# Eight of the q transposes move from TensorE and ScalarE to a crossbar DMA on SyncE, with a new order table

## The chip, the cores and the metric

The kernel runs on one core of a Trainium2 chip. The metric is the device time of one execution in microseconds (us). The engines are named as in the profile: PE is TensorE (PEld is its weight load), DVE is VectorE, ACT is ScalarE, POOL is GpSimd, SP is SyncE. PE, DVE, ACT and POOL compute; SP only issues DMAs here, and ACT and POOL issue some as well.

## What is computed

A linear attention over 8 batches, 8 heads, 576 positions and 64 channels per head feeds a channel mix with 512 model channels and 1024 hidden ones. The inputs and the output are float32; the matmuls run in bfloat16.

```python
# attention: q, k, v are [8, 8, 576, 64]
q_s = softmax(q, axis=-1)            # over the 64 channels
k_s = softmax(k, axis=2)             # over the 576 positions
kv  = einsum('bhsd,bhse->bhde', k_s, v)
x   = einsum('bhsd,bhde->bhse', q_s, kv)        # then [8, 576, 512]
# channel mix
x_prev = x shifted by one position (a zero in front)
xk = mu_k * x + (1 - mu_k) * x_prev
xr = mu_r * x + (1 - mu_r) * x_prev
k  = relu(xk @ w_k)                  # [.., 1024]
out = sigmoid(xr @ w_r) * (k * k @ w_v)
```

## The kernel before

The kernel is a list of some 950 operations (`Op`), each with an engine, what it depends on and which buffers it takes and gives. A long string, `ORDER` (L42 to L115), names all of them in one sequence; `Plan.ordered` (L149) emits them in that sequence. Each engine then runs its own operations strictly in the order in which the table has them, and waits at an operation until its inputs are there. The number after a colon is the buffer that the operation takes. `ACT!load00k0` puts a DMA on ACT's queue. So the table decides what stands behind what on every engine and on every DMA queue, and nothing is reordered at run time.

The names are made of a kind and indices. For the attention the indices are batch and group of four heads (two groups a batch), so `qt41` is batch 4, group 1:

- `load41q0`, `load41k0`, `load41v0`: the loads (L189 to L205), for batches 1 to 7 on POOL's queue.
- `expq`, `rsum`, `rrec`, `scale` (L419 to L422): exp of q on ACT, then row sums, reciprocals and the scaled softmax on DVE, which writes q into a tile `qs` [128, 9, 128]: a partition holds one head of a pair and one of 64 rows of positions, the free dimension nine blocks of 128 channels (two heads of 64).
- `expk`, `cast` (L423, L425): exp of k and the cast of v, on ACT.
- `B41` (L440 to L448), one block on PE with three parts in a row: x of the head group before it (`x`, L512 to L519, which reads that group's transposed q from `qt` and its weights `w`), the transposes of this group's q (`transpose_q`, L356 to L363: for batches 4 to 7 36 matmuls of 64 by 64 against an identity, into PSUM), and this group's `kv` (L383 to L392). `TKV20` and `TKV30` are blocks without the first part; for the two groups in `ALONE` the x is a block of its own (`X21`, `X71`).
- `rz`, `w` (L451, L506) on DVE: one over the sum of exp(k), and the weights kv over it.
- `qt41` (L507, `copy_qt` L365 to L372): ACT copies the transposed q from PSUM into the SBUF tile `qt` [128, 2, 640]. It waits for `B41` and for `w41`, and gives the PSUM pair back.
- `xs`, `xb` on ACT, `edge`, `diff`, `sc`, `mix` on DVE (L521 to L556): x out of PSUM, its shift and the two mixes xk and xr.

The channel mix runs over 10 units of 512 positions (two of them, units 4 and 9, of 256), index first: `k46` is unit 4, hidden block 6 (L598; four matmuls, PE), `relu46` (ACT) and `sq46` (DVE) follow it; `r40` and `th40` are the gate of unit 4, tile 0 of 128 positions (L630, PE; tanh on ACT); `v400` and `v401` are the two halves of its second matmul (L650, PE, four matmuls each); `o40` multiplies the two (L657, DVE) and gives `th`, of which there are 7 buffers; `st40` and `st40.2` store its two halves of 64 positions from SP's queue (L662). Of the last unit, `v910`/`v911` and `v910.2`/`v911.2` are the two column halves of the last tile, `o91` and `o91.2` their gates; for the last two tiles the second store of each pair (`st90.2`, `st91.2`, `st91.4`) is issued by ACT (L680).

Batches 0 and 1 are treated in another way (`FUSED`: the mixing factors are put into the weights); the change doesn't touch them, nor batches 2 and 3, except for their places in the table.

Of the kernel before, what the change touches and what calls it, by code (L numbers as in the profile page):

```python
# [38 lines left out]
ALONE = ((2, 1), (B - 1, 1))  # L39
FIRST = ((0, 0), (0, 1), (1, 0), (1, 1))  # L40

ORDER = """  # L42
ACT!load00q0:0 zero ident load00q1 ACT!load00k0:1 load01q1:2 ACT!load01q0 rows load00v consts warm
load00k1 load01v late load01k0:3 load10q0:4 wk00 load11q0:5 expq001:0 wk01 expq000 rsum001:0 wk10
rsum000 expk000:0 wk11 ACT!load01k1 rrec001 rrec000 scale001:0 expq011:1 scale000 fill:1 fill.2:2
fill.3:3 fill.4:0 fill.5:1 fill.6:2 fill.7:3 fill.8:0 fill.9:1 fill.10:2 fill.11:3 fill.12:0
fill.13:1 fill.14:2 fill.15:3 fill.16:0 wide:0 expq010 rsum011:1 fill.17:1 fill.18:2 T00:0 rsum010
expk001 load10q1 rrec011 rrec010 scale011:1 widecopy fill.19:3 KV001:1 qt00:0 KV000 scale010 Z00
fill.20:1 fill.21:1 T01:3 rz00:0 rest expk010:1 kvn00:0 expk011 edge00 load10k0:6 fill.22:1
KV010:2 wp000:0 expq100:2 wp001 wr X000:0.1 qt01:1 KV011 x0001 Z01 load11q1 x0000 rz01:1 X001:1.3  # L50
kvn01:1 load10v1:7 edge01 k00:0 wp010:1 x0010 k02:1 x0011 expq110:0 X010:0.1 wv0 k01:2 x0100 x0101
k03:3 wp011 load10k1 k00.2 k02.2 relu00:0 k03.2 load10v0 relu02:1 k01.2 relu03:2 k05:0 load11v0:8
sq02:0 sq00 relu01:1 load11v1 k04:1 relu05:0 sq01 expq101 rsum100:2 k07:3 expk100:2 rrec100 sq03
X011:0.1 relu07:1 load11k1:9 k06:2 x0110 x0111 load11k0 relu04:2 sq05 r03:0 scale100:2 relu06:0
wv1 expq111 rsum101 r00:3 cast101:0 rsum111:3 r02:1 th03:0 rrec111 th00:1 rrec101 rsum110 r01:2
th02:2 wv2 rrec110 expk101 v020:0 sq04 load20v0:10 scale111:0 cast100 v030:3 load20q0:0 scale101
th01:3 sq07 muload v000:1 cast110:1 scale110 cast111 TKV10:0 expk111:0 load21q0:2 v010:2 rz10:2
expk110 kvn10:0 sq06 qt10:2 wp100:0 TKV11:1 v021 rz11:0 kvn11:1 v011 qt11:0 wp110:1 wp111 v001
# [12 lines left out]
rz30:0 k23:2 sc2111:1 st10 sc2110 st10.2 th20:1 mix211 load50k0:3 k22:0 cast400:0 w30:2 o13 k27:3
relu23:2 scale310:1 load61q0:8 st13 k24:1 relu22:1 st02.2 qt30:2 st13.2 k21:2 rsum400:0 st01
relu24:0 k20:0 st12.2 expk400:2 sq22:0 st12 mix201 B31:0.1 relu21:1 sq24 load51k0:9 r22:1 xs30:1
rz31:1 sq23 relu27:0 rrec400 w31:0 relu20:2 r23:2 scale400:2 xb30 k25:3 qt31:1 sq27 edge30 k26:0
sq21 diff30:0 relu25:0 B40:1.0 relu26:1 sc3001:2 sq25 expq410:0 r21:3 sq20 rz40:2 w40:1 th23:6
sq26 load71k0:1 v230:0 rsum410:1 th21:2 th22:0 v200:2 xs31:0 xb31 sc3000 v220:3 sc3011:1 sc3010
mix300 qt40:0 r30:1 edge31 diff31:1 expq500:1 v201 sc3101:0 v221 sc3100 th30:4 load51v0:2 mix310
cast410:1 v231 o22 expk410:0 k35:1 sc3110:2 load61k0:6 o23 k33:3 rrec410 st23.2 relu35:0 o20
load70v0:0 expq510:2 rsum500:2 k30:0 st20.2 st11.2 k41:1 load70q0:7 st01.2 sq35:1 v210:2 relu41:2
sc3111 st23 cast500:2 scale410:0 k37:1 relu33:1 load70k0:4 v211 mix301 relu37:0 expk500:1 k32:3  # L80
sq41:0 o21 k40:1 expq600:0 sq37 load60k0:3 st21 k31:2 sq33 st21.2 rrec500 mix311 relu40:2 B41:0.1
load71v0:10 relu31:0 rsum510:3 relu32:1 r32:1 sq40 sq32 r33:2 relu30:2 rrec510 scale500:1 th32:3
r31:3 xb40:1 sq30 k36:0 xs40 sq31 th31:6 edge40 scale510:2 k34:1 relu36:1 k47:3 relu34:2 diff40:0
v310:0 th33:2 sq34 expk510:2 v330:1 rz41:0 sc4001:0 w41:2 sc4010:1 v300:2 relu47:0 sq36 load71q0:9
rsum600:0 k46:3 v331 relu46:2 cast510:0 sq46 k44:3 sc4000 rrec600 v311 mix400 relu44:1 load61v0:2
qt41:2 scale600:0 k43:3 v301 expq610:1 o31 B50:1.0 relu43:2 o30 r41:0 sc4011 xs41:0 st30.2 rz50:1
xb41 sq47 w50:0 st31 k42:3 st31.2 v320:2 edge41 relu42:0 st11 diff41:1 qt50:1 st30 k45:3 sq44
sc4101:2 st20 v321 cast600:1 o33 sc4100 B51:0.1 sq43 relu45:1 mix410 cast610:2 r40:1 sq42 rz51:2
sq45 o32 expq700:2 k52:3 rsum610:1 th41:6 k50:2 relu52:2 sc4111:0 k51:0 rrec610 relu50:0 rsum700:2
expk600:0 v410:3 sq52:1 k53:2 relu51:1 sc4110 w51:1 expk610:1 sq51 v411 mix411 relu53:2 k54:0 o41  # L90
xb50:0 sq50 v400:2 scale610:1 relu54:1 k55:3 expq710:0 rrec700 mix401 v401 relu55:0 rsum710:3
th40:5 k56:0 qt51:0 k57:3 sq53 sq54 relu56:2 r50:1 sq55 relu57:1 scale700:2 r51:0 th50:4 cast700:0
rrec710 v500:3 o40 sq56 st40 v510:1 th51:1 sq57 st41 xs50 edge50 B60:1.0 st33 diff50:0 st32.2 v501
st41.2 xb51:1 sc5000:2 rz60:0 sc5001 st40.2 w60:2 v511 mix500 xs51 qt60:2 o50 r52:2 expk700:2 o51
st50 B61:0.1 edge51 st50.2 sc5010:0 expk710:0 diff51:1 st22 v520:0 st51 sc5011 th52:6 sc5100:1
st51.2 r53:3 sc5101 cast710:1 sc5110:2 mix510 v521 sc5111 th53:5 rz61:1 mix511 v530:1 o52 xb60:1
k60:2 w61:0 st52 mix501 qt61:1 v531 st32 scale710:0 st52.2 k61:3 relu60:0 st22.2 xs60 o53 B70:1.0
relu61:2 sq60:0 st53 edge60 k62:0 st53.2 diff60:0 xb61:0 st33.2 sq61 k63:2 sc6000:1 relu62:1
sc6001 sc6010:2 xs61 k64:1 mix600 relu63:0 sq62 k65:3 relu64:2 edge61 sq63 diff61:1 k66:0 relu65:1
sq64 k67:2 sc6100:0 relu66:0 sc6101 sq65 r60:1 mix610 relu67:2 sq66 r61:3 th60:4 sc6011 sq67  # L100
# [12 lines left out]
sq94 k97:2 relu96:0 sq95 r90:1 relu97:2 sq96 sq97 r91:0 th90:5 v900:3 th91:2 v901 v910:2 o90 v911
st90.2 st90 v910.2:1 o91 v911.2 st91.2 st91 o91.2 st91.4 st91.3
"""  # L115


class Slot:

# [698 lines left out]
```

## Time and profile before

| | |
|---|---|
| median of 3 runs | 198.74 us (198.21 to 198.87) |
| the profiled execution's own time | 198.64 us |
| its span, first to last instruction | 196.9 us |
| DVE busy | 150.6 us (77%), 347 instructions |
| ACT busy | 147.0 us (75%), 224 instructions |
| POOL busy | 43.5 us (22%), 70 instructions |
| DMA bytes moved | 40.13 MB, HBM read 33.56 MB, written 9.44 MB |
| mean granted clock of PE | 0.995 |

What lies around the span is 198.64 - 196.9 = 1.7 us. DVE and ACT are busy over 90% of most of the first two thirds and much less in the last third; the DMA engines are full up to about 75 us, and again in part up to 95 us, and carry little but stores after that.

### The profile page before, as it was taken

What the parts mean: (1) busy time and instruction counts of PE and PEld (TensorE: products, weight loads), DVE (VectorE), ACT (ScalarE), POOL (GpSimd) and SP (SyncE); (2) the same over time, 40 slices, a digit from 0 to 9 for tenths busy, and PEclk for the clock granted to TensorE, in tenths of its full rate; (3) what the DMA queues carried; (4) which work ended last, traced back from release to release, by engine and by line L of the source; (5) the groups of instructions that cost most, each with busy time, mean ns of one, the idle gap of its engine ahead of it and who ended that gap; (6) DMA issues with size and microseconds to landing.
All of it is one profiled execution on the core that took longest, in us unless ns stands there. A gap on an engine that the chain in (4) does not pass through costs nothing.

```text
span 196.9 us, 5187 instructions
## 1 busy us (share of the span) xinstructions
PE 189.0 (96%) x2089; PEld 92.4 (47%) x2089; DVE 150.6 (77%) x347; ACT 147.0 (75%) x224; POOL 43.5 (22%) x70
## 2 busy tenths in 40 slices
PE   7799999999999999999999999999999999999992
PEld 3263445444544554454455445554444544444751
DVE  1985796899999899999799999999725459622531
ACT  3786989899999999998789997986525762652440
POOL 8533456983415202440110000000000000000000
PEclk9999999999999999999999999999999999999998
DMA  6999999999999997799284004653044013403413
GB/s 201 307 294 263 269 358 307 390 384 389 416 392 394 403 409 291 176 410 415 56 268 114 0 0 114 158 127 89 3 107 107 0 42 70 107 0 87 97 34 107
DMA packets 16544, 40.13 MB, mean 204 GB/s; under 512 B 2300, under 2 KB 5640, under 8 KB 16520
## 3 DMA queue, kind: packets, MB, share of 16 engines
q0 software_dynamic: 9440, 27.99, 43.1%
q1 hardware_dynamic: 6264, 10.36, 19.5%
q10 hardware_dynamic: 816, 1.44, 2.0%
q8 instruction: 16, 0.26, 0.5%
q14 instruction: 8, 0.07, 0.1%
HBM read 33.56 MB, written 9.44 MB: 218 GB/s over the span
## 4 chain that ended last, share of the span: by engine, by line
PE 66%; DMA 15%; DVE 8%; ACT 4%; POOL 3%; issue 1%; SPq 0%; DVEq 0%; POOLq 0%; ACTq 0%
PE mm_c L652 10%; PE mm_d L652 8%; PE mm_d L600 7%; DMA wk_bb<-in_moe_w_k_dram 7%; PE mm_a L600 6%; PE mm_c L600 5%; PE mm_b L632 5%; DMA raw_h<-in_v_dram 5%; PE mm_b L600 5%; PE mm_a L652 5%; DMA out_dram<-th_c 4%; PE mm_a L632 4%; PE mm_b L652 3%; PE mm_d L632 2%; PE att_b L390 1%
## 5 line engine op out<-in xcount | busy, mean ns | idle before, releaser
L652 PEld LDWEIGHTS <-k_a 128*128 128x128 bf16 x144 | 13.7, 98 | 16.6 <-DMA wv_a<-in_moe_w_v_dram 0.4
L652 PEld LDWEIGHTS <-k_b 128*128 128x128 bf16 x152 | 14.3, 98 | 14.4 <-issue 0.8
L632 PEld LDWEIGHTS <-xr 128*128 128x128 bf16 x144 | 13.6, 98 | 15.6 <-DVE xr L488 0.2
L632 PE MATMUL mm_b<-wr,xr 128*128 128x512 bf16 x56 | 14.4, 380 | 0.0
L600 PEld LDWEIGHTS <-wk_ba 128*128 128x128 bf16 x80 | 7.7, 98 | 9.1 <-issue 0.8
L600 PEld LDWEIGHTS <-wk_ab 128*128 128x128 bf16 x80 | 7.7, 98 | 8.2 <-issue 0.8
L600 PEld LDWEIGHTS <-wk_bb 128*128 128x128 bf16 x80 | 7.8, 98 | 7.7
L600 PEld LDWEIGHTS <-wk_aa 128*128 128x128 bf16 x80 | 7.5, 98 | 8.2 <-issue 0.7
L632 PE MATMUL mm_a<-wr,xr 128*128 128x512 bf16 x36 | 9.3, 380 | 0.0
L652 PE MATMUL mm_c<-wv_a,k_a 128*128 128x512 bf16 x32 | 8.2, 379 | 0.0
L591 DVE TENSOR_TENSOR k_b<-rel_b 128x512 bf16<-128x512 bf16 (+1 forms) x15 | 6.0, 402 | 2.1 <-ACT rel_b L587 1.8
L600 PE MATMUL mm_d<-xk,wk_ba 128*128 128x512 bf16 (+1 forms) x28 | 7.3, 341 | 0.3 <-ACT rel_a L587 0.3
L591 DVE TENSOR_TENSOR k_a<-rel_b 128x512 bf16<-128x512 bf16 (+1 forms) x13 | 5.2, 398 | 3.0 <-ACT rel_b L587 3.0
L600 PE MATMUL mm_d<-xk,wk_bb 128*128 128x512 bf16 (+1 forms) x28 | 7.3, 341 | 0.0
L632 PE MATMUL mm_d<-wr,xr 128*128 128x512 bf16 x28 | 7.2, 379 | 0.0
L587 ACT ACTIVATE rel_c<-mm_b 128x512 bf16<-128x512 f32 (+1 forms) x7 | 3.6, 509 | 4.7 <-PE mm_b L600 4.7
L600 PE MATMUL mm_c<-xk,wk_aa 128*128 128x512 bf16 (+1 forms) x24 | 6.9, 371 | 0.0
L600 PE MATMUL mm_c<-xk,wk_ab 128*128 128x512 bf16 (+1 forms) x24 | 6.9, 370 | 0.0
L587 ACT ACTIVATE rel_a<-mm_b 128x512 bf16<-128x512 f32 (+1 forms) x7 | 4.2, 593 | 3.6 <-PE mm_b L600 3.6
L591 DVE TENSOR_TENSOR k_a<-rel_c 128x512 bf16<-128x512 bf16 (+1 forms) x14 | 5.2, 372 | 1.9 <-ACT rel_c L587 1.9
L600 PE MATMUL mm_a<-xk,wk_aa 128*128 128x512 bf16 (+1 forms) x22 | 6.4, 370 | 0.1
L600 PE MATMUL mm_a<-xk,wk_ab 128*128 128x512 bf16 (+1 forms) x22 | 6.3, 369 | 0.1
(346 smaller groups left out, 545.9 us busy)
## 6 DMA issues: line engine op xcount, KB each, us to landing
raw_d<-in_k_dram POOLq DMA_DIRECT2D x4, 576.0 KB, 10.0
out_dram<-th_g SPq DMA_DIRECT2D x14, 128.0 KB, 2.4
raw_c<-in_q_dram POOLq DMA_DIRECT2D x3, 576.0 KB, 9.8
raw_h<-in_q_dram POOLq DMA_DIRECT2D x3, 576.0 KB, 9.9
out_dram<-th_a SPq DMA_DIRECT2D x10, 128.0 KB, 7.3
out_dram<-th_b SPq DMA_DIRECT2D x10, 128.0 KB, 2.4
out_dram<-th_e SPq DMA_DIRECT2D x10, 128.0 KB, 2.4
raw_k<-in_v_dram POOLq DMA_DIRECT2D x2, 576.0 KB, 7.9
```

The costliest lines, as they stand in the source:

```text
L390: kn.nc.tensor.matmul(kn.half(slot, r)[two[u], KVO:KVO + n], lhsT=kn.eks[ek.index][two[r], j, u, :], rhs=by, start=(j == 0), stop=(j == J ...
L587: kn.nc.scalar.activation(out=kn.rels[rel.index][:, 0:n], in_=kn.bank(kf)[:, 0:n], func=ACT.Relu, scale=HALF_ROOT)
L591: kn.nc.vector.tensor_tensor(out=kn.k2s[k2.index][:, fc, 0:n], in0=kn.rels[rel.index][:, 0:n], in1=kn.rels[rel.index][:, 0:n], op=ALU.mult)
L600: kn.nc.tensor.matmul(kn.bank(kf)[:, 0:n], lhsT=kn.wk[fc // 4][ct % 2][:, ct // 2, (fc % 4) * 128: (fc % 4) * 128 + 128], rhs=kn.xs[0][:, ...
L632: kn.nc.tensor.matmul(kn.bank(rps), lhsT=kn.xs[1][:, ct, c:c + 128], rhs=kn.wr[:, ct, :], start=(ct == 0), stop=(ct == CT - 1))
L652: kn.nc.tensor.matmul(kn.bank(vps)[:, 0:width], lhsT=kn.k2s[k2.index][:, ft, 128 * m:128 * m + 128], rhs=wv_of(ft)[:, part], start=(ft == ...
```

## The change

For batches 4 to 7 (`CROSSBAR`, eight head groups) the transposes leave the PE block, and ACT's copy `qt` is replaced by one DMA on SP's queue, which reads the whole tile `qs` [128, 9, 128] and writes its nine 128 by 128 blocks transposed into the tile `qt`. The DMA waits for the scaled q (`scale`) and for the `qt` buffer. The PE block no longer waits for `scale`; the block that reads the transposed q, the next one of the list, now waits for the DMA. The PSUM pair is given back by `w` instead of by the copy. The layout of the transposed tile differs: x of these groups reads eight runs of 64 columns, 128 elements apart, instead of 512 columns in a row. The table `ORDER` is new as a whole; in it most stores stand right behind their `o`.

```diff
+CROSSBAR = tuple((b, g) for b in range(4, B) for g in range(2))
 ORDER = """
...
+qt41:2 r31:1 sq31:0 relu37:2 o20 st20 st20.2 k32:3 rz41:0 sq35
+th31:2 rsum500:2 k33:0 relu32:1 xb40:1 k46:2 w41:2 sq37 k30:1 sq32 xs40 relu33:0 edge40 k40:3
+rrec500 rsum510:3 r32:0 relu40:2 relu30:1 k34:3 th32:5 sq30 sq33 B50:0.1 diff40:0 relu34:1 k42:1
...
+v821 relu96:2 v830:0 o82 st82 st82.2 sq95 v811 sq96 v800:3 o81 st81 st81.2 sq92 v831 v801 v910:2
+o80 st80 st80.2 v900:1 o83 st83 st83.2 v910.2:3 v911 v901 v911.2 o90 o91.2 st90 o91 st91.2 st91
+st90.2 st91.4 st91.3
 """
...
+        def qt_crossed(t):
+            return t[:].rearrange("p r c -> p (r c)")[:, 0:2 * S].rearrange(
+                "p (j c) -> p j c", c=128)
...
+        crossed = (b, g) in CROSSBAR
...
-                transpose_q(qtp)
+                if not crossed:
+                    transpose_q(qtp)
                 kv(qtp)
...
-                tr = kvm = add("PE", block, before_t + before_kv + turn_x[1] + alone, [qtp] + turn_x[2], [qs] + leave_kv + turn_x[3], name=f"B{tag}")
+                tr = kvm = add("PE", block, ([] if crossed else before_t) + before_kv + turn_x[1] + alone, [qtp] + turn_x[2], ([] if crossed else [qs]) + leave_kv + turn_x[3], name=f"B{tag}")
...
-        wdone = add("DVE", lambda: weights(kvp, kn.ws[w.index]), [zdone], [w], [rz], name=f"w{tag}")
-        qcopy = add("ACT", lambda: copy_qt(qtp), [tr, wdone], [qt], [qtp], name=f"qt{tag}")
+        wdone = add("DVE", lambda: weights(kvp, kn.ws[w.index]), [zdone], [w], [kvp, rz] if crossed else [rz], name=f"w{tag}")
+        if crossed:
+            qcopy = add("SP", lambda: kn.nc.sync.dma_start_transpose(
+                out=qt_crossed(kn.qts[qt.index]),
+                in_=kn.qss[qs.index][:].rearrange("p j d -> p (j d)")), scaled, [qt], [qs],
+                name=f"qt{tag}")
+        else:
+            qcopy = add("ACT", lambda: copy_qt(qtp), [tr, wdone], [qt], [qtp], name=f"qt{tag}")
...
+        def x_columns(r, u, at, n):
+            t = kn.qts[qt.index]
+            if crossed:
+                return qt_crossed(t)[two[u], at // 64:(at + n) // 64, 64 * r:64 * r + 64]
+            return t[two[u], r, 64 + at:64 + at + n]
```

The end of the table before reads `v900 th91 v901 v910 o90 v911 st90.2 st90 v910.2 o91 v911.2 st91.2 st91 o91.2 st91.4 st91.3` (buffer numbers left out).

More of the change, by code (lines that the diff above doesn't have):

```diff
@@ L39 @@
 ALONE = ((2, 1), (B - 1, 1))
+CROSSBAR = tuple((b, g) for b in range(4, B) for g in range(2))
 FIRST = ((0, 0), (0, 1), (1, 0), (1, 1))
 ORDER = """
[L43 to L46, printed above, removed]
@@ L53 @@
[L53 to L58, printed above, removed]
@@ L71 @@
[L71 to L100, printed above, removed]
@@ L113 @@
-sq94 k97:2 relu96:0 sq95 r90:1 relu97:2 sq96 sq97 r91:0 th90:5 v900:3 th91:2 v901 v910:2 o90 v911
-st90.2 st90 v910.2:1 o91 v911.2 st91.2 st91 o91.2 st91.4 st91.3
+ACT!load00q0:0 zero load00v load00q1 ACT!load00k0:1 load01q1:2 ident ACT!load01q0 rows
+ACT!load00k1 load01k0:3 load01v consts warm load10k1:4 late wk00 load10q1:5 expq001:0 load01k1
+expq000 wk01 rsum001:0 rsum000 wk11 expq011:1 rrec001 expk000:0 wk10 rrec000 scale001:0 fill:1
+fill.2:2 fill.3:3 fill.4:0 fill.5:1 fill.6:2 fill.7:3 fill.8:0 fill.9:1 fill.10:2 fill.11:3
@@ new lines @@
+relu01:1 k03.2 X011:1.0 load10k0 relu03:2 k07:0 load10v0 x0110 x0111 expq100 sq01:0 k05:1 sq02
+relu00:1 k04:3 sq00 relu05:0 relu07:1 load11v0:9 r00:2 sq05 expq110:0 load11k0 r01:1 expq111
+load11v1 r02:0 th00:0 rsum111:3 wv1 cast101:0 r03:2 rrec111 relu04:0 rrec101 sq03 rsum110 th01:1
+k06:3 th02:2 rrec110 scale101:2 th03:3 v010:1 wv2 relu06:2 rsum100 expk111:0 v030:0 load20v0:10
+rrec100 sq04 expk100 sq07 muload v020:2 scale100 cast100 v000:3 scale111:0 cast110:1 load20q0:0
+scale110 TKV10:0 expk110 load21q0:2 sq06 cast111 rz10:2 load30q0:1 kvn10:0 qt10:2 TKV11:1 v001
@@ new lines @@
+mix210 v131 rz30:0 o10 cast310:2 load70v0:7 sc2110:0 k23:2 st10.2 o13 st12 load50v0:10 sc2111
+k27:1 relu23:1 st02 scale310:1 th20:4 st02.2 k20:3 relu27:2 st03.2 w30:2 cast400:0 k21:2 st12.2
+sq27:0 sq23 mix201 k24:0 qt30:2 load50k0:0 rsum400:0 k26:1 relu21:0 relu20:2 B31:1.0 mix211
+expk400:2 rrec400 k22:2 sq20 rz31:1 relu24:1 sq21 load51v0:8 scale400:2 relu26:2 k25:3 relu22:0
+r22:0 xs30:0 w31:0 xb30 qt40:0 sq24 sq22 r23:1 qt31:1 edge30 r21:2 diff30:0 th22:2 st01 sc3001:2
+B40:0.1 th21:3 sq26 sc3010:1 v220:0 relu25:1 sc3000 th23:6 sq25 r30:2 expq410:0 sc3011 mix300 v221
@@ new lines @@
+xs31:1 rsum410:1 load60q0:5 xb31 v230:3 th30:1 edge31 v210:1 cast410:1 diff31:1 v231 rz40:2
+sc3101:0 expq500:1 load60k0:3 sc3100 o22 st22 st22.2 v211 expk410:0 mix310 load71v0:4 v200:2 w40:1
+sc3110:2 expq510:2 st10 k35:0 o23 st23 st23.2 load71k0:1 o21 st21 st21.2 v201 load61q0:9 relu35:0
+sc3111 cast500:2 mix311 k31:3 rrec410 mix301 k41:1 expk500:1 load61v0:10 B41:1.0 scale410:0 k37:0
+relu41:2 load70k0:0 relu31:1 sq41:1 qt41:2 r31:1 sq31:0 relu37:2 o20 st20 st20.2 k32:3 rz41:0 sq35
+th31:2 rsum500:2 k33:0 relu32:1 xb40:1 k46:2 w41:2 sq37 k30:1 sq32 xs40 relu33:0 edge40 k40:3
@@ new lines @@
+st33 st33.2 relu45:0 expq700:2 rsum610:1 k53:2 k52:1 rrec600 sq42 sq47 relu53:2 k55:3 sq45
+scale600:0 relu52:1 v410:2 relu55:0 rz51:2 cast600:1 sc4110:0 k51:1 mix401 sq52:0 k57:3 o32 st32
+st32.2 relu51:1 v411 sq55 expq710:0 sc4111 sq53 k54:0 sq51 xs50:1 qt51:0 relu57:0 o41 st41 st41.2
+k50:1 xb50 mix411 rsum700:2 k56:3 relu50:2 r40:2 relu56:1 rrec700 edge50 r50:1 w51:1 th40:0 sq50
+diff50:0 r51:3 rsum710:3 r53:2 qt60:2 th51:6 relu54:2 sc5011:1 B60:0.1 sq57 sc5010 v500:3 xs51:0
+sq56 th50:4 sq54 xb51 rz60:0 r52:0 sc5001:2 v400:1 edge51 th52:5 diff51:1 cast610:2 v501 sc5000
@@ new lines @@
+rrec710 rrec610 v530:0 w60:2 th53:3 mix501 cast700:0 v510:2 mix500 sc5100:0 expk610:1 v401
+sc5111:1 sc5101 o50 st50 st50.2 v511 sc5110 mix510 v531 o40 st40 st40.2 k63:3 o53 st53 st53.2
+scale610:1 k62:1 relu63:0 expk700:2 k61:0 o51 st51 st51.2 qt61:1 k60:3 cast710:1 scale700:2
+B61:1.0 relu61:1 sq63:1 v520:2 relu62:2 qt70:0 rz61:1 sq61 relu60:0 scale710:0 k64:0 xb60:1 k67:1
+mix511 xs60 w61:0 k66:3 relu67:1 B70:0.1 sq67 qt71:2 edge60 sq60 r60:1 xs61:0 relu64:1 rz70:2
+w70:1 xb61 v521 sq64 sq62 diff60:0 th60:1 k65:0 edge61 o52 st52 st52.2 r62:1 relu65:0 sc6010:2
@@ L517, in x @@
                                             lhsT=kn.ws[w.index][two[u], r, :],
[L518 removed]
+                                            rhs=x_columns(r, u, at, n),
                                             start=True, stop=True)
```

66 lines of the change are left out of this document (35 added, 31 removed).

## The prediction

> **What bounds the kernel now.** I read first the busy shares, then the 40 slices, PE's waits, the stretches of 5 us, and the timeline of one block that the change touches.
>
> ```profile
> PE 189.0 (96%) x2089; PEld 92.4 (47%) x2089; DVE 150.6 (77%) x347; ACT 147.0 (75%) x224; POOL 43.5 (22%) x70
> ...
> PE   7799999999999999999999999999999999999992
> ```
>
> PE is busy in all slices but the first two and the last. Its waits between 33 and 190 us are two:
>
> ```profile
> PE mm_d L600 <- ACT rel_a L587: 0.3, 1, 0.3
> PE att_b L390 <- ACT ek_a L325: 0.3, 1, 0.3
> ```
>
> So from 33 us on PE's own work sets the end: a microsecond of PE work taken out there is a microsecond gained, and a new wait of PE there is lost in full. Before 33 us the loads set the pace. The end of the chain of waits into block TKV11 shows it: ACT's last exp follows the loads, and PE waits for it.
>
> ```profile
> 31.45 0.58 ACT ek_a L325
> 32.05 0.69 ACT ek_a L325
> 32.79 0.48 PE att_b L390 x36
> ```
>
> **What is removed: PE.** One block, B50 (start, duration, instruction):
>
> ```profile
> 100.01 0.22 PE L516 MATMUL att_b<-qt_c,w_c 64*64 64x64 bf16 x4
> 100.06 0.39 PE L516 MATMUL att_a<-qt_c,w_c 64*64 64x512 bf16 x4
> 100.28 0.46 PE L360 MATMUL att_b<-ident,qs_b 64*64 64x64 bf16 x36
> 100.56 0.48 PE L390 MATMUL att_b<-vv_c,ek_b 64*64 64x65 bf16 x36
> 100.97 1.04 PE L632 MATMUL mm_a<-wr,xr 128*128 128x512 bf16 x4
> ```
>
> Matmuls are pipelined, so a part costs the distance of the starts, not its duration: the 36 transposes cost 100.56 - 100.28 = 0.28 us. The eight blocks (starts at 71.55, 87.31, 100.28, 104.81, 120.55, 124.36, 131.59 and 156.10) give 0.28 to 0.30 each, in sum 2.29 us, all in the stretch where PE has no gaps. Gain: 2.29 us, certain to within 0.1.
>
> **What is removed: ACT.** Eight copies like this group's:
>
> ```profile
> L368 ACT COPY qt_a<-att_b 128x1152 bf16<-128x1152 bf16 x4 | 4.6, 1152 | 1.3 <-DVE w_b L407 1.1 <-DVE kvn_b L407 0.2
> ```
>
> 8 x 1.13 = 9 us of ACT, and its wait for `w` (1.1 us once). I count it at 0: PE's work covers ACT, and it waited 0.3 us for ACT in 157 us. If a dearer order needed ACT sooner it could be worth those 0.3 us.
>
> **What is added: eight transposing DMAs.** The trace has none. Each moves 128 x 1152 x 2 = 288 KB within SBUF. The nearest rows, from issue to landing:
>
> ```profile
> out_dram<-th_a SPq DMA_DIRECT2D x10, 128.0 KB, 7.3
> out_dram<-th_b SPq DMA_DIRECT2D x10, 128.0 KB, 2.4
> ...
> raw_f<-in_q_dram POOLq DMA_DIRECT2D x2, 288.0 KB, 10.9
> ...
> raw_c<-in_q_dram SPq DMA_DIRECT2D x1, 288.0 KB, 4.7
> ```
>
> Bounds: not under 2.4 us (a store of under half the bytes, alone) and, by the same bytes in a crowd of loads, up to 10.9. Alone on the DMA engines I take 3.3 us: 2.4 plus 160 KB at 204 GB/s, the page's mean (0.8; rounded up). Beside loads, as up to 95 us, I take 6 us: stores of 128 KB in flight between 78 and 95 us have medians of 3.3 to 7.5, several queued at once, and this one stands nearly alone with over twice the bytes.
>
> The Trainium skill speaks for both ends. "DMA: Bandwidth & Descriptors" (section "Latency and other measured facts") has 261 GB/s for a transposing DMA, an estimate of 1.1 us for these bytes plus the fixed part. "VectorE: DVE Perf Modes" (section "The three transpose paths") has 1,309 ns for one 128 by 128 block by DMA against 390 on TensorE, and advises TensorE where PSUM will do; nine blocks one after another would be 11.8 us. No run here shows either; the second is the case of the slow transposes below.
>
> **How much time each transpose has.** A full PE step (four matmuls of 512 columns) is 0.86 us, a half one 0.44, by the chain of waits. DVE steps there: scale 1.27, mix 0.67, o 0.59, sc 0.28, rrec 0.17. The new table's own sequences tell which is short.
> - qt61 stands on SP behind the stores of o51. From the end of v531 DVE has o53, scale610, o51: 0.59 + 1.27 + 0.59 = 2.45 us. PE has k63, k62, k61, k60, k64, k67, k66 and then B70, which reads qt61: 7 x 0.86 = 6.0. Left: 3.6 us.
> - qt41 waits for scale410. From the end of v211 DVE has up to mix310, w40, sc3110, o23, o21, sc3111, mix311, rrec410, mix301, scale410, some 5.4 us; PE has five steps of which one is half (3.9), B41 (0.68 without transposes) and k37, r31, k32, k33, k46, k30, k40, r32, k34 (6.9) before B50: 11.5. Left: 6.1 us, at about 83 to 89 us, beside the last loads.
> - qt51 stands behind the stores of o32, about 5.5 us ahead of B60 (k50, k56, r40, r50, r51, r53 and a little). The others have 6 to 15 us, by the PE steps between.
>
> At 3.3 us alone and 6 us beside loads all fit, by 0.3 and 0.1 us. So: 0, with 0.1 us for the narrow ones. Each microsecond more costs one at B70 and one at B50; from 5.5 us on a third at B60. At the low bound still 0.
>
> **What is moved.** SP issues 85 DMAs instead of 77: the eight are added and each holds the queue for 0.5 to 1.7 us (the issues of stores). Queued behind a waiting transpose are stores, and for them only the next tanh on one of 7 `th` buffers waits; two stores take 2.4 us and a tile 3 PE steps. I count 0; if the queue jams by 5 us, a tanh comes late and PE with it. The 1 us of DMA time each is 8 us of 16 engines that carry 85 GB/s after 95 us.
>
> x reads eight runs of 64 columns instead of 512. Low bound 0; high, if each run costs as the matmuls of 64 columns above do (0.05 for four), 8 x 0.05 against 0.22, 0.18 x 8 = 1.4 us. I take 0: the same columns stream, in the same number of matmuls.
>
> **The start and the middle under the new table.** Up to TKV11 the new sequence on POOL brings the same loads, only load11v1 last instead of load11k0, and PE has the same steps to do; one cast instead of two exps stands behind the last load. I take 0, with -0.7 to +0.7. From there to B31 the PE steps are the same in number. A new table may leave PE gaps that no row tells: 0 to 2 us.
>
> **The end.** Start, duration, instruction of the last microseconds:
>
> ```profile
> 192.55 0.38 PE L652 MATMUL mm_b<-wv_c,k_b 128*128 128x256 bf16 x2
> ...
> 192.64 1.40 ACTq L668 DMA_DIRECT2D out_dram<-th_c  x2
> 192.97 0.42 DVE L658 SCALAR_TENSOR_TENSOR th_c<-th_c,mm_b 128x256 f32<-128x256 f32 x1 [0.40 <-PE mm_b L652]
> ```
>
> PE ends at T = 192.93; one half-width o follows (to T + 0.46), then the last issue (0.70, the second of the two), and it lands 2.2 us after that (the median of these stores), at T + 2.7. The new table ends PE with v901, v911.2 and DVE with o90, o91.2, o91, in this order: v901 is done 0.44 before T, o90 (0.69) runs to T + 0.3, o91.2 to T + 0.6, o91 to T + 1.0. ACT then issues st91.2, st90.2, st91.4 one after another, 0.70 each: the last at T + 2.4 at most, landed at T + 4.4 or a little later. Loss: 1.7 us (1.3 to 2.1).
>
> **Sum**, against the profiled execution's 198.64 (0.1 under the median of 198.74): 198.64 - 2.29 + 1.7 + 0.1 = 198.15, and with the 0.1 of the median about 198.2. Under 0.3% (0.6 us) a measurement of this kernel can't be told from no change; this sits 0.5 below the median.
>
> **The rivals.**
> 1. *The transposes come late* (slower). Place: B70 and B50, which wait for qt61 and qt41, with all of PE behind them. It decides from 3.6 us alone and 6.1 beside loads. At 5 us and 7.5: 1.4 + 1.4, 198.2 + 2.8 = 201.0; a range of 199 to 202. For it: margins of 0.3 and 0.1 us, and stores beside loads take up to 7.5. Against: from 95 us on the DMA engines are mostly free.
> 2. *The transposes go block by block*, at the 10.9 us of the highest row: B50 4.8, B60 5.4, B70 7.3 late, 198.2 + 17.5 = 215.7; at 8 us 207. Against: nothing else in the kernel is as slow with so little queued.
> 3. *The gain stays whole*: the end costs less (o91 not held by o90, ACT's issues closer) and ACT's freed 9 us close PE's small waits: 198.7 - 2.3 + 0.8 - 0.3 = 196.9. For it: ACT is full up to 95 us. Against: in-order queues at the end.
> 4. *Gaps of the new table* of 1 to 2 us elsewhere on PE: 199.2 to 200.2.
> That the change doesn't do what it says is excluded: PE's program has 288 matmuls less.
>
> **How the numbers follow.** Forecast 0.45 (own range 197.6 to 198.9), rival 1 0.25, rival 2 0.08, rival 3 0.12, rival 4 0.10. Faster by over 0.3% (below 198.14): half of the forecast's case (0.22) and rival 3: 0.34. Same: the other half less its edge, 0.2, and the mild parts of 1 and 4, 0.08: 0.28. Slower: 0.38. The range reaches from rival 3 to the upper part of rival 1: 197.0 to 201.6, which leaves out rival 2 and a few hundredths below.
>
> **What would show it.** B blocks of batches 4 to 7 at 0.68 us instead of 0.96. Transposes landing in 3.3 us alone; if 5 or more, the starts of B70 and B50 show PE waiting for them. The last landing 4.4 us after PE's last matmul. It is wrong if PE has new waits over 1 us between 33 and 190 us that no transpose explains, if x (L516) takes more than 0.27 a block, or if the start shifts TKV11.

## The result, and the profile after

The changed kernel takes 206.76 us (median of 4 runs, 206.35 to 207.11) where the kernel before took 198.60 (198.21 to 198.87): a ratio of 1.041, with a 95% interval of 1.038 to 1.044. It is slower by 8.2 us, and lies 5 us above the upper end of the predicted range. The profiled execution took 206.64 us, its span is 204.9. Medians here and below are of all runs of a kernel, while ratios leave out the runs that are over 1.5% above its fastest.

First the page of the changed kernel: the busy shares, PE's row and the row of its granted clock in 40 slices of 5.1 us, and the DMA packets.

```profile
PE 190.4 (93%) x1801; PEld 92.5 (45%) x1801; DVE 149.3 (73%) x346; ACT 137.1 (67%) x217; POOL 43.7 (21%) x70
...
PE   7789999999999899991999999999999999999980
...
PEclk9957999999999999998599999999999999999996
...
DMA packets 26013, 42.44 MB, mean 207 GB/s; under 512 B 11772, under 2 KB 15112, under 8 KB 25992
```

The last two of these rows in the kernel before:

```profile
PEclk9999999999999999999999999999999999999998
...
DMA packets 16544, 40.13 MB, mean 204 GB/s; under 512 B 2300, under 2 KB 5640, under 8 KB 16520
```

PE has 288 instructions less (2089 to 1801), as it should, and yet 1.4 us more busy time, since it ran at a lower clock in the third and fourth slice and in the 19th and 20th. In the 19th it is nearly idle. The small packets went from 2300 to 11772: 9472 more, 1184 for each of the eight new DMAs.

PE's waits from 25 to 200 us, longest first (what waited, for what, us in total, times, longest):

```profile
PE att_a L536 <- DMA qt_c<-qs_a: 4.7, 1, 4.7
PE att_b L536 <- ACT qt_c L374: 0.6, 1, 0.6
```

The first is block B50, which waits for the transpose qt41. The timeline of PE there (start, duration, instruction, idle time before it):

```profile
97.52 0.27 PE L536 MATMUL att_a<-qt_c,w_c 64*64 64x64 bf16 x4 [4.65 <-DMA qt_c<-qs_a]
97.55 0.67 PE L536 MATMUL att_b<-qt_c,w_c 64*64 64x512 bf16 x4
97.96 0.75 PE L396 MATMUL att_a<-vv_c,ek_b 64*64 64x65 bf16 x36
98.64 0.61 PE L620 MATMUL mm_b<-xk,wk_aa 128*128 128x256 bf16 x2
...
99.47 0.64 PE L620 MATMUL mm_a<-xk,wk_ba 128*128 128x256 bf16 x2
...
100.32 0.63 PE L620 MATMUL mm_d<-xk,wk_ba 128*128 128x256 bf16 x2
```

Between x (L536) and kv (L396) nothing stands any more: the transposes are gone. But behind the wait PE runs at half its pace. Three half-width k steps start at 98.64, 99.47 and 100.32, 0.84 us apart; at full clock such a step takes 0.44. The busy time in stretches of 5 us shows the granted clock (third number from the end) beside it:

```profile
90.00:95.00 5.00, 2.86 (x16) 1.37 (x14) 5.00 (x11) 2.85 (x7) 0.00 (x0) 1.00 1.03 318
95.00:100.00 5.00, 2.48 (x51) 1.85 (x51) 0.97 (x4) 0.84 (x3) 0.00 (x0) 0.60 1.04 298
100.00:105.00 5.00, 5.00 (x23) 2.59 (x22) 1.62 (x4) 3.31 (x6) 0.72 (x1) 0.72 0.22 43
```

Taken finer, the granted clock is 1.00 up to 95.9 us, 0.50 from 96.0 to 102.7 and 1.00 again from 102.9, so the two lower figures are averages over a stretch of half clock.

The Trainium skill, "TensorE: Matmul & The Clock Gate" (Part 1, the HAM clock gate), says that PE falls back to half its clock after an idle stretch of about 3.4 us; with 4.65 us of idle and a clock of 0.60 and 0.72 behind it, this trace agrees.

SP's queue around qt41 (SPq: issuing; start, how long the issue holds the queue):

```profile
84.14 1.22 SPq L688 DMA_DIRECT2D out_dram<-th_d  x2
86.56 5.13 SPq L516 DMA_TRANSPOSE qt_c<-qs_a  x1
91.79 1.51 SPq L688 DMA_DIRECT2D out_dram<-th_e  x2
95.45 1.28 SPq L516 DMA_TRANSPOSE qt_b<-qs_b  x1
```

qt41 was issued at 86.56 and landed at 97.47, 10.9 us later, and its issue alone held SP's queue for 5.1 us. In flight meanwhile were the loads 71v, 71k, 61q, 61v and 70k (landed at 88.4, 91.6, 93.5, 95.2 and 96.8). The issues of the whole run, with the median time from issue to landing:

```profile
qt_a<-qs_c SPq DMA_TRANSPOSE x3, 3.4
qt_c<-qs_a SPq DMA_TRANSPOSE x3, 3.4
qt_b<-qs_b SPq DMA_TRANSPOSE x2, 3.5
```

So five of the eight took 3.3 to 3.4 us, and qt50, beside the end of the last of these loads, 3.7; only qt40 (6.3) and qt41 (10.9) stood beside loads for most of their time. A median hides the one that counts.

The end, from PE's last matmuls to the last issue:

```profile
198.70 0.38 PE L672 MATMUL mm_d<-wv_c,k_a 128*128 128x256 bf16 x2
...
199.62 0.41 DVE L678 SCALAR_TENSOR_TENSOR th_g<-th_g,mm_c 128x256 f32<-128x256 f32 x1
...
201.51 0.61 ACTq L688 DMA_DIRECT2D out_dram<-th_g  x1
```

From PE's last end (199.08) to the span's end (204.9) are 5.8 us, against 3.9 before: 1.9 us more, and the last of three issues of ACT in a row is at the end of it.

Where the blocks start, in us, shows what was lost by when (B40 and later stand among other steps in the new table, and don't compare one to one):

| | before | after | difference |
|---|---|---|---|
| TKV11 | 32.07 | 34.14 | +2.1 |
| TKV20 | 46.91 | 48.41 | +1.5 |
| B31 | 66.62 | 68.77 | +2.15 |
| last v911.2 | 192.33 | 198.48 | +6.15 |
| end of span | 196.9 | 204.9 | +8.0 |

### The profile page after: what moved, and what is told of

Same layout as the page of the kernel before. It is cut to its first block, busy times and chain, and to the rows that moved or that the text cites. A ratio compares the mean times of both kernels' runs of the same rounds, so it can differ in the third digit from the quotient of the medians.

```text
span 204.9 us, 4601 instructions
## 1 busy us (share of the span) xinstructions
PE 190.4 (93%) x1801; PEld 92.5 (45%) x1801; DVE 149.3 (73%) x346; ACT 137.1 (67%) x217; POOL 43.7 (21%) x70
## 2 busy tenths in 40 slices
DMA packets 26013, 42.44 MB, mean 207 GB/s; under 512 B 11772, under 2 KB 15112, under 8 KB 25992
## 3 DMA queue, kind: packets, MB, share of 16 engines
HBM read 33.56 MB, written 9.44 MB: 210 GB/s over the span
## 4 chain that ended last, share of the span: by engine, by line
PE 76%; DMA 13%; DVE 5%; ACT 2%; ACTq 1%; issue 1%; SPq 1%; DVEq 0%
PE mm_d L620 8%; PE mm_c L672 8%; PE mm_a L620 7%; PE mm_a L672 7%; PE mm_b L672 7%; PE mm_d L672 6%; PE mm_b L620 6%; DMA qt_c<-qs_a 5%; PE mm_c L620 5%; PE mm_c L652 4%; DMA raw_b<-in_k_dram 4%; PE mm_b L652 3%; DMA out_dram<-th_e 3%; PE mm_a L652 3%; PE mm_d L652 2%; PE att_a L486 1%
## 5 line engine op out<-in xcount | busy, mean ns | idle before, releaser
L672 PEld LDWEIGHTS <-k_a 128*128 128x128 bf16 x184 | 17.5, 98 | 19.3 <-issue 0.7
L652 PE MATMUL mm_c<-wr,xr 128*128 128x512 bf16 x48 | 12.3, 379 | 0.0
L652 PE MATMUL mm_b<-wr,xr 128*128 128x512 bf16 x40 | 10.3, 379 | 0.0
L607 ACT ACTIVATE rel_b<-mm_a 128x512 bf16<-128x512 f32 (+1 forms) x8 | 4.4, 547 | 8.4 <-PE mm_a L620 8.3
L611 DVE TENSOR_TENSOR k_b<-rel_a 128x512 bf16<-128x512 bf16 (+1 forms) x13 | 4.9, 380 | 6.7 <-ACT rel_a L607 6.7
L611 DVE TENSOR_TENSOR k_a<-rel_a 128x512 bf16<-128x512 bf16 (+1 forms) x15 | 6.0, 397 | 4.5 <-ACT rel_a L607 4.5
L607 ACT ACTIVATE rel_a<-mm_d 128x512 bf16<-128x512 f32 x9 | 5.4, 601 | 4.2 <-PE mm_d L620 2.7
L620 PE MATMUL mm_a<-xk,wk_ba 128*128 128x512 bf16 (+1 forms) x28 | 7.8, 360 | 0.0
L620 PE MATMUL mm_a<-xk,wk_bb 128*128 128x512 bf16 (+1 forms) x28 | 7.7, 359 | 0.0
L620 PE MATMUL mm_b<-xk,wk_ab 128*128 128x512 bf16 (+1 forms) x26 | 7.1, 358 | 0.0
```

The lines of the kernel that those rows point to most:

```text
L607: kn.nc.scalar.activation(out=kn.rels[rel.index][:, 0:n], in_=kn.bank(kf)[:, 0:n], func=ACT.Relu, scale=HALF_ROOT)
L611: kn.nc.vector.tensor_tensor(out=kn.k2s[k2.index][:, fc, 0:n], in0=kn.rels[rel.index][:, 0:n], in1=kn.rels[rel.index][:, 0:n], op=ALU.mult)
L620: kn.nc.tensor.matmul(kn.bank(kf)[:, 0:n], lhsT=kn.wk[fc // 4][ct % 2][:, ct // 2, (fc % 4) * 128: (fc % 4) * 128 + 128], rhs=kn.xs[0][:, ...
L652: kn.nc.tensor.matmul(kn.bank(rps), lhsT=kn.xs[1][:, ct, c:c + 128], rhs=kn.wr[:, ct, :], start=(ct == 0), stop=(ct == CT - 1))
L672: kn.nc.tensor.matmul(kn.bank(vps)[:, 0:width], lhsT=kn.k2s[k2.index][:, ft, 128 * m:128 * m + 128], rhs=wv_of(ft)[:, part], start=(ft == ...
```

## The experiments

Theory 1 at the start: the transposing DMA is harmless where it has time; qt41 was slow since it stood behind stores in its queue; the rest is the table's start and end. The rivals stand with each run. Times are medians; the kernel before, on the same chip as each run, had 198.5 to 199.0.

**The old table with the DMA.** Only the change of mechanism, without the new sequence (qt41's place is shown; the other seven are moved in the same way):

```diff
-... scale410:0 k37:1 ... load61v0:2 qt41:2 scale600:0 ...
+... scale410:0 qt41:2 k37:1 ... load61v0:2 scale600:0 ...
```

> The table of the kernel before, with the eight transposes done by the DMA on SP's queue, each placed right behind its scale (or behind the block that frees its buffer). Nothing else of the new table is used. Theory 1 (the transposing DMA is harmless where it has time; the loss comes from the place of one of them in the new table, and from the table's start and end): the 2.29 us of PE come out whole, 198.6 - 2.3 = 196.3 us, no wait of PE for qt, and the start and the tail as before (TKV11 at 32.1 us, 3.9 us from the last matmul to the end). Rival (the transposing DMAs themselves disturb the loads or wait for them wherever they stand): 198.6 us or more, with loads landing later than before and waits of PE for them or for qt. Rival 4 of the prediction, the other way round (the old table was tuned for the copies, so PE finds new gaps): between, 197 to 198.5.

Measured: 203.63 us (201.83 to 210.64), ratio 1.021 (1.016 to 1.026); the profiled run took 204.92. Theory 1 fell here, and with it my blame on the table alone. Start and tail are as before, and PE waits for no qt. But qt40 took 13.2 us, qt41 14.7 and qt50 8.1, and their issues held SP's queue:

```profile
82.39 0.59 SPq L686 DMA_DIRECT2D out_dram<-th_d  x1
...
84.51 5.15 SPq L514 DMA_TRANSPOSE qt_c<-qs_a  x1
89.76 2.90 SPq L686 DMA_DIRECT2D out_dram<-th_c  x2
92.83 5.58 SPq L514 DMA_TRANSPOSE qt_b<-qs_b  x1
```

Stores came late at two places, and so did the two tanhs that want their buffers. ACT's timeline of the same run:

```profile
92.69 0.60 ACT L655 ACTIVATE th_d<-mm_b 128x512 f32<-128x512 f32 x1 [3.31 <-DMA out_dram<-th_d]
99.88 0.60 ACT L655 ACTIVATE th_c<-mm_c 128x512 f32<-128x512 f32 x1 [4.04 <-DMA out_dram<-th_c]
```

The second tanh waits for stores that stood behind qt41 in the queue: they were issued at 89.8 and 92.0 (85.7 and 86.2 before) and landed just after qt41 (99.2). The store of the first was issued at 82.4, ahead of qt41 (82.1 before), and landed at 92.6 instead of 89.4; it was late without standing behind qt41. PE then waits for the tanhs (1.9, 1.6 and 0.6 us) and loses clock again, 0.50 from 95.2 to 98.6 and from 102.0 to 105.5, though from 25 us up to the first fall no wait was longer than the 1.9 us. B50, 100.0 us before, starts at 107.5.

**qt41 ahead of the stores.**

```diff
-... st22 st22.2 ... st10 ... st23 st23.2 ... st21 st21.2 ... qt41:2 r31:1
+... qt41:2 st22 st22.2 st10 st23 st23.2 st21 st21.2 r31:1
```

> The changed kernel with seven stores (of o22, o23, o21 and one old one) moved from ahead of the transpose qt41 to behind it on SP's queue. Theory 1 (qt41 took 10.9 us because it stood in its queue behind stores that share the DMA engines with the loads): qt41 lands within 6.5 us of its issue, PE has no wait at B50, and no lower clock after it: 206.7 - 4.65 - 2.3 = 199.7 us. Rival (the loads alone slow a transposing DMA of this size there): qt41 still needs 9 to 11 us, the wait at B50 stays at 4 to 5 us, 206 to 207 us.

Measured: 213.7 us (209.0 to 216.7), the worst of all: its fastest run is slower than every run of the changed kernel. In the profiled run (212.9) qt41 took 13.1 us with no store ahead of it, so the stores ahead were not what made it slow. And the seven stores, now behind it, landed after it (99.7 to 101.6). ACT's timeline:

```profile
100.17 0.60 ACT L655 ACTIVATE th_c<-mm_b 128x512 f32<-128x512 f32 x1 [12.46 <-DMA out_dram<-th_c]
```

The Trainium skill, "DMA: Bandwidth & Descriptors" (section "Queues, rings and completion order"), says that each DMA engine takes the descriptors of one queue in their order; a store behind a transpose that waits is then late as well, and this run agrees: the tanh began 0.8 us after qt41 had landed (99.4).

**PE kept busy in the wait.**

```diff
-FILLS = 22
+FILLS = 42
...
-... th32:5 sq30 sq33 B50:0.1
+... th32:5 sq30 sq33 fill.23:0 fill.24:1 ... fill.42:1 B50:0.1
```

> The changed kernel with 20 matmuls that compute nothing of use put on PE just ahead of B50, where it waits for qt41, so that PE isn't idle in the wait. Theory (the clock granted to PE falls to 0.60 and 0.72 in the two stretches of 5 us behind the wait because PE was idle in it): B50 starts within 0.5 us of where it did (97.5 us), the clock stays near 1.00, and the half-speed steps are gone: 206.7 - 2.3 = 204.4 us. Rival (the lower clock has another cause, or the steps behind the wait were slow for another reason): 206.5 to 207.5 us and the same clock dip.

Measured: 204.64 us (203.90 to 206.34), 2.1 less than the changed kernel. x in B50 started at 97.76, 0.24 later, and the clock stayed at 1.00:

```profile
95.00:100.00 5.00, 5.00 (x71) 2.93 (x70) 1.67 (x5) 1.35 (x5) 0.00 (x0) 1.00 1.12 236
```

In the two profiles the next block, B51, starts 9.44 us after B50 instead of 11.90, which is 2.5 us. So a wait of 4.65 us cost 6.75 by the medians and 7.1 by the profiles: the second price is the clock.

**The old end of the table.**

```diff
-... v910:2 o80 st80 st80.2 v900:1 o83 ... v901 v911.2 o90 o91.2 st90 o91 st91.2 st91 st90.2 st91.4 st91.3
+... v900:1 o83 ... v901 v910:2 o80 ... o90 v911 st90.2 st90 v910.2:3 o91 v911.2 st91.2 st91 o91.2 st91.4 st91.3
```

> The changed kernel with the last operations in the order of the table before: o90, o91, o91.2 and the stores of the last two tiles, with v910 and v911 ahead of their second halves. Theory (the tail is 1.85 us longer through the order of o90, o91.2, o91 and three stores issued by ACT in a row): 3.9 to 4.1 us from the last matmul to the end instead of 5.8, 206.7 - 1.8 = 204.9 us. Rival (the tail is set by the stores of the tiles before, which stand later in the new table): under 0.5 us gained.

Measured: 204.93 us (203.91 to 205.97), 1.83 less, as expected. In its profile the end, from PE's last end, takes 3.9 us instead of 5.8.

**Old table, six groups and five groups.**

```diff
-CROSSBAR = tuple((b, g) for b in range(4, B) for g in range(2))
+CROSSBAR = ((5, 0), (5, 1), (6, 0), (6, 1), (7, 0), (7, 1))
...
+CROSSBAR = ((5, 1), (6, 0), (6, 1), (7, 0), (7, 1))
```

> The table of the kernel before, with the DMA for the six groups of batches 5 to 7 alone; batch 4 is transposed on PE again. In the run with all eight, the transposes beside the loads took 13.2 (qt40), 14.7 (qt41) and 8.1 us (qt50), the others 3.2 to 3.4, and PE first fell behind after qt41, where stores queued behind it came late to a tanh. Theory 2 (a transposing DMA is slow beside loads, 74 small packets on each of 16 engines, each of which has to let a load packet pass; what PE loses comes from qt41 alone, through SP's queue): without batch 4 PE loses nothing, 198.65 less 6 x 0.285 = 196.9 us; qt50 takes 4 to 8 us at the end of the loads and harms nothing. Rival (qt50 beside the last loads also holds the stores up, or each DMA costs something wherever it stands): 198 us or more.

> As the run with batches 5 to 7, but group 0 of batch 5 too on PE: only the five transposes that stand behind the last load are DMAs. Theory 2: 198.65 less 5 x 0.285 = 197.2 us, all five in 3.2 to 3.4 us. Rival (each DMA costs something wherever it stands, in x or on SP's queue): 198.4 us or more.

Measured: 197.24 us with six, ratio 0.993 (0.991 to 0.994), and 197.06 with five, 0.992 (0.990 to 0.994). Both are faster than the kernel before. With five, PE's waits from 33 to 190 us are those of the kernel before and no others:

```profile
PE mm_d L618 <- ACT rel_a L605: 0.3, 1, 0.3
PE att_b L394 <- ACT ek_a L325: 0.3, 1, 0.3
```

The five DMAs took 3.2 to 5.9 us, the longest of them (qt60) beside the last load, which is issued at 98.7, behind the 95 us up to which I had counted loads. At these places a DMA costs nothing that the runs show and saves its 0.28 us. The sixth (qt50, 6.1 us) brought nothing that these runs could tell.

**Loads held during qt41.**

```diff
-... load71k0:1 ... load61q0:9 ... load61v0:10 ... load70k0:0 ... qt41:2
+... qt41:2 load71k0^qt41:1 load61q0^qt41:9 load61v0^qt41:10 load70k0^qt41:0
```

The `^` adds a wait: the load is issued when qt41 has landed.

> The changed kernel with four loads (71k0, 61q0, 61v0, 70k0), which it issues just before qt41, held on POOL until qt41 has landed; the stores ahead of qt41 stay where they were. Theory 2 (the loads slow the transposing DMA): qt41 lands 3.5 to 5 us after its issue instead of 10.9, no wait at B50, no lower clock behind it; the held loads have 10 us and more to spare: 206.7 - 4.65 - 2.1 = 199.9 us. Rival (the stores in its own queue, or the instruction itself at that place, make it slow): qt41 still 9 us or more and 206 us.

Measured: 205.27 us (202.46 to 206.46). In the profiled run (205.64) qt41 took 6.2 us, still with the stores and the end of the loads under way beside it, and the wait at B50 was gone: B50 started at 93.97 instead of 97.52. But the held loads then ran beside the next transpose:

```profile
qt_c<-qs_a SPq DMA_TRANSPOSE x1, 6.2
qt_b<-qs_b SPq DMA_TRANSPOSE x1, 9.8
```

(issues between 86 and 107 us). qt50, 3.7 us in the changed kernel, took 9.8, and B51 waited for it:

```profile
106.48 0.22 PE L535 MATMUL att_b<-qt_b,w_a 64*64 64x64 bf16 x4 [3.00 <-DVE xk L563]
```

The view names DVE, whose last operation happened to end at 106.44; what B51 needs of DVE was done at 102.7, and qt50 landed at 106.44. The wait moved along with the loads. That is the strongest evidence that the loads make it.

**The first loads as before.**

```diff
-... ACT!load00k1 load01k0:3 ... expq001:0 load01k1 expq000 ... expk000:0
+... load00k1 load01k0:3 ... expq001:0 expq000 ... expk000:0 ACT!load01k1
```

> The changed kernel with two of the first loads on the queues that they had before (load00k1 on SP, load01k1 on ACT behind expk000). Theory (the start is 1.5 us late at TKV20 because load00k1, as the fourth on ACT's queue, lands 1.3 us later and PE idles into a lower clock): KV001 at 9.7 us instead of 11.0, the clock back at 1.00 between 10 and 20 us, TKV20 at 46.9 instead of 48.4, 206.7 - 1.5 = 205.2 us. Rival (the order of the other start operations and loads sets it): under 0.4 us gained at TKV20.

Measured: 205.51 us (205.32 to 207.10; the profiled run is the slowest). The reason failed: KV001 started at 11.2, not 9.7, since its exp stands on ACT behind one that waits for load01q0 (9.4). The clock was at 1.00 in this profile and TKV20 at 47.2, but B31 was no earlier (69.3), so in this run what the start gained was lost again between TKV20 and B31. The median is 1.25 us lower all the same; the three faster runs left no profile, so where they gained it stays open.

**One group back on PE, then three repairs together.**

```diff
+CROSSBAR = ((4, 0), (5, 0), (5, 1), (6, 0), (6, 1), (7, 0), (7, 1))
...
-... B41:1.0 scale410:0 k37:0 ... qt41:2 r31:1 ... w41:2 sq37
+... scale410:0 k37:0 ... r31:1 B41:1.0 ... w41:2 qt41:2 sq37
```

> The changed kernel with one of the eight groups, batch 4 group 1, transposed on PE and copied by ACT again (its block B41 two PE steps later, behind the scale that it needs). Theory 2 (the whole loss behind 85 us is qt41 beside the loads, and the clock after the wait for it): no wait at B50, clock 1.00 there, 206.7 - 4.65 - 2.1 + 0.3 = 200.2 us. Rival (with that wait gone another takes its place, as qt50 did at B51 when the loads were held): 202 us or more.

> As the run with one group back on PE, and also the end of the table and the two first loads as in the kernel before. If the three causes add up: 200.2 - 1.8 - 1.3 = 197.1 us, that is under the kernel before by about what the seven removed transposes are worth (2.0), less 0.6 at B31. Rival (the start's gain is given back at B31, as the run with the old start loads alone showed in its profile): 198.4 us.

The three repairs are this one, the old end of the table and the old places of the two first loads. Measured: 200.98 us and 200.06. The first took away 5.8 us with a single one of the eight transposes: qt41 is the main cause in the changed kernel. The second missed by 3 us. In its profile the start and the end were repaired only in part: the clock is low again from 10.8 to 17.7 us, TKV20 starts at 48.2, and the end takes 4.8 us instead of the 3.9 of the old end alone; one of the last stores took 3.6 us there, 2.6 with the old end alone. And something was still hidden. ACT's timeline of the first shows it:

```profile
65.65 0.60 ACT L655 ACTIVATE th_e<-mm_a 128x512 f32<-128x512 f32 x1 [2.73 <-DMA out_dram<-th_e]
```

The tanh th20 takes buffer 4 (th_e) in the new table, whose store st11.2 was issued at 57.3 and, beside the loads, landed at 65.5. Behind it B31 starts at 68.8, though TKV20 had started at 46.8; in the nine profiles of the new table with this order B31 starts at 67.7 to 69.3, with TKV20 anywhere from 46.8 to 48.9.

**Old table, seven groups.** All but batch 4 group 1 (`CROSSBAR` as in the last diff).

> The table of the kernel before with the DMA for all groups of batches 4 to 7 but batch 4 group 1. Theory 2 (beside loads a transposing DMA is long, 13 us for qt40 in the run with all eight, but that costs only where its reader or the stores behind it are short of time, which is qt41 alone): 198.55 less 7 x 0.285 = 196.5 us. Rival (the long DMAs qt40 and qt50 hold SP's queue and cost what they bring): 197.1 us or more, as with five groups.

Measured: 197.69 us, ratio 0.992 (0.989 to 0.995), but from 196.25 to 201.22 over 12 runs. The fastest gives the expected 196.5 (196.25), eight more lie between 196.7 and 199.1, three above 200. The profile is of the fastest: there qt40 took 10.4 us and qt50 7.2, and PE waited for nothing new. What held the slow runs up no profile shows; that it was the long DMAs beside the loads is a guess.

**The late stores repaired.**

```diff
-... st03 expq300:0 ... th20:4 ... st03.2 ... th21:3
+... st03 st03.2 expq300:0 ... th20:3 ... th21:4
```

> As the run with one group back on PE, with the tanh th20 on buffer 3 (and th21 on 4), and the store st03.2 moved right behind st03, so that buffer 3 is free long before. In four profiles of the new table th20 began at 65.4 to 65.7 us, just as the store st11.2 of its buffer landed beside the loads, and B31 at 67.9 to 69.3, whether the start had been fast or slow. Theory (this store sets B31, and takes back what a fast start gains): th20 at about 63 us, B31 at 66.8 to 67.3 with a fast start (TKV20 at 46.8) and 68.3 with a slow one, up to 1.7 us gained: 201.0 - 1.7 = 199.3 us, less with slow starts among the runs. Rival (ACT's own work there sets B31): B31 stays at 68.8, 201 us.

> As the run before, with the old end of the table and nine more of the matmuls that only keep PE busy in the first 11 us. Theory (the start is slow where PE's idle time of about 1 us ahead of T00 and KV001 lowers its clock to 0.56 and 0.75; kept busy, it isn't): TKV20 at 47.0 us with the clock at 1.00 from 5 to 25 us, and with the tail repaired 201.0 - 1.7 - 1.0 = 198.3 us; were the tail's whole 1.8 us to come, 197.5. Rival (the lower clock at the start has another cause): the clock falls there all the same, TKV20 at 48.3, 199 us.

Measured: 202.34 and 200.16 us. B31 moved as expected, to 67.4 (with TKV20 at 47.7) and 67.0 (47.3), 19.7 us behind TKV20 as in the kernel before, but the time did not. The first is even 1.4 us slower than without the repair; in its profile PE waits 0.6 and 1.35 us at 84 and 86 us, and the clock is at 0.50 from 87.0 to 90.4. In the second, ACT's timeline has the next wait:

```profile
78.82 0.60 ACT L656 ACTIVATE th_b<-mm_c 128x512 f32<-128x512 f32 x1 [2.27 <-DMA out_dram<-th_b]
```

This is th30, whose store st01 stands right behind the transpose qt40 on SP's queue.

At the start the nine more fills kept PE busy, and its clock stayed at 1.00. These are the stretches of the changed kernel from 10 to 20 us:

```profile
10.00:15.00 5.00, 4.21 (x86) 2.40 (x87) 3.08 (x11) 3.35 (x5) 1.85 (x3) 0.56 1.15 302
15.00:20.00 5.00, 5.00 (x91) 2.76 (x86) 3.71 (x11) 3.59 (x8) 1.83 (x3) 0.75 1.21 233
```

and these those of the run with four repairs:

```profile
10.00:15.00 5.00, 5.00 (x151) 3.02 (x149) 3.43 (x13) 3.94 (x7) 1.78 (x3) 1.00 1.14 296
15.00:20.00 5.00, 4.68 (x68) 2.22 (x63) 4.51 (x13) 3.07 (x7) 2.16 (x5) 1.00 1.21 236
```

Of ten profiles of the new table without them seven show the lower clock there, of two with them none. That fits, but two profiles don't prove it.

**A fifth repair: st01 forward.**

```diff
-... st03 st03.2 expq300:0 ... th22:2 st01 ...
+... st03 st03.2 st01 expq300:0 ... th22:2 ...
```

> As the run with four repairs, with one more store, st01, moved forward to just behind st03.2; in the new table it stands on SP's queue right behind the transpose qt40. In all profiles of the new table st01 landed at 78.0 to 78.8 us, and the tanh th30 (on its buffer, th_b) waited for it: 2.3 us of ACT in the run with four repairs, and PE then waited 1.4, 0.7 and 0.6 us for ACT's relu. Theory (a store behind a transposing DMA beside loads comes late to a tanh, at qt40 as at qt41): th30 at 76.6 us, those three waits gone, B41 at 85.5 to 86 us instead of 87.5: 200.2 - 1.7 = 198.5 us. Rival (ACT has more work there than it can do before B41): the waits stay, 200 us.

Measured: 197.81 us, ratio 0.996 (0.995 to 0.998). The wait is gone, B41 starts at 85.0 instead of 87.5, and 2.35 us came with it. With these five repairs the new table is faster than the kernel before, by 0.9 us. PE's last step ends 1.8 us earlier (191.1 against 192.9), about what seven transposes are worth (2.0), but the end takes 4.8 us instead of 3.9, as with the three repairs.

**Loads in halves.**

```diff
-        us = [slice(0, 1), slice(1, 2)] if b < 2 else [slice(0, 2)]
+        halves = b < 2 or (b, g, i) in ((7, 1, 2), (7, 1, 1), (6, 1, 0), (6, 1, 2), (7, 0, 1))
+        us = [slice(0, 1), slice(1, 2)] if halves else [slice(0, 2)]
...
```

> The changed kernel with the five loads around qt41 (71v, 71k, 61q, 61v, 70k) as two DMAs each, so that a packet of them has half as many bytes; the bytes are the same. What is told apart is why a transposing DMA is long beside loads. By turns of packets (each of its 74 packets on an engine lets one packet of the loads pass): 74 times about 0.10 us and its own 1.5, some 9 us instead of 10.9 to 11.5. By order of arrival, or by bytes alone: it lands when the loads ahead of it have landed, 11 us as before, or later with the five more issues on POOL.

Measured: 208.26 us in one run, qt41 12.1 us. It tells nothing on turns of packets: from 80 to 102 us POOL's queue moved 4.06 MB in 1073 packets, against 4.01 MB in 982 in the changed kernel, so its packets were hardly smaller (3.8 KB against 4.1). By what rule the engines share their time between the transposes and the loads stays open.

## Why the prediction was wrong, point by point

- *The removal of the transposes, 2.29 us*: right. The blocks take 0.68 us from x to kv's end; with five groups in the old table PE's last step came 1.2 us earlier, 1.5 when a start 0.3 later is counted, against 5 x 0.285 = 1.4.
- *3.3 us alone*: right (3.2 to 3.5 at most places with no load beside, 3.6 to 4.6 at some). The nine blocks are not done one after another at the Trainium skill's 1,309 ns ("VectorE: DVE Perf Modes", "The three transpose paths"): nine in 3.3 us is 0.37 each.
- *6 us beside loads, since it "stands nearly alone"*: the step that failed. Up to five loads of 576 KB stood beside it, and it took 10.9; with four of them held back it took 6.2. That 10.9 is just the upper bound that I had named and not taken is chance: at the same place it took 11.2 to 11.5 in three other runs, and 14.7 in the old table. The margin itself was right: 6.1 us reckoned, 6.3 in the trace. The loss, 4.65 us at B50, is rival 1 in mechanism and place, at more than its price.
- *SP's queue, counted at 0 unless it "jams by 5 us"*: wrong. It jammed by 5.1 to 5.6 us, and what came late was a tanh, as the prediction said; I did not see that this would occur. In the old table it accounts for one of the two late tanhs, in the new one it is hidden until the larger waits are gone.
- *The clock*: no term of the sum held it. It cost 2.1 us behind B50 by the medians, 2.5 by the profiles.
- *The middle, 0 to 2 us*: B31 came 2.15 us late. 1.5 of it was lost by TKV20, with the lower clock, where I took 0; the other 0.65 came between TKV20 and B31, where the tanh th20 starts at 65.57, just behind the landing of its buffer's store at 65.47. Where the start was earlier, that tanh took back most of the gain. So rival 4 came true as well, on top.
- *The end, 1.7 us*: right, 1.83 by the medians of the run that undoes it, 1.9 by its profile.
- *x in eight runs of 64 columns, 0*: right, 0.27 us at full clock, as before.
- *ACT's 9 us less, 0*: right as far as the runs show; five groups gained 1.45 us, which PE's part (1.4) covers.

The sum with the measured terms: 198.6 - 2.3 + 4.65 + 2.1 + 2.15 + 1.8 = 207.0, against 206.76. That it comes so close is partly luck: up to the last v911.2 the same terms make 6.6 us, where the table of starts has 6.15.

## What to carry to other kernels

The time of a DMA is not its own: ask which transfers share the engines with it and which stand behind it on its queue, and where a row shows the crowded price, take that one. A mechanism that fails at one of eight places can still pay at others: here it was best at the five that are far from most loads, 197.06 us against 206.76, while with seven the runs went up to 201.2. Each wait removed may uncover the next, so undo causes together before concluding that one of them was not a cause; and put a second price, the clock, on every PE wait of several microseconds.

## What the runs showed of the hardware

- A transposing DMA of 288 KB within SBUF makes 1184 packets under 512 B. With no loads beside it, it takes 3.2 to 3.5 us at most places and up to 4.6 at some; with loads of 576 KB beside it, it took from 3.7 (the end of a single one) to 14.7 (seven of them). Its issue holds SP's queue for 1.3 us, and beside loads for up to 6.1. Where stores stood right behind it in the same queue and qt41 took 13.1 and 14.7 us, they landed after it.
- The granted clock of PE was 0.50 from 96.0 to 102.7 us behind a wait of 4.65 us (0.60 and 0.72 in stretches of 5 us), and it fell to 0.56 and 0.75 from 10 to 20 us, where PE had waited 0.9 us before its step at 9.1 and 0.8 us before that at 11.0; there it did so in some runs and not in others. In the old table with the DMA it fell to 0.50 behind waits of 1.9 and 0.6 us.
- A store of 128 KB took 8.2 us beside the loads (st11.2 with one group back on PE, 57.3 to 65.5) where such stores take 2.4 later on.
